# An attention backward kernel: transposing e by one DMA per unit instead of one per two units, with the plain loads and stores on another queue

## Chip, cores and metric

The kernel runs on one core of one Trainium2 chip. The metric is the time of an execution on the device in microseconds (us). One run of the kernel before took 3037.18 us and is left out of every ratio. A ratio is the mean time of one kernel's fast runs over that of the other's of the same rounds on the same chip, so it is not quite the ratio of the medians that are quoted beside it. Each profile is of one of four runs.

## The reference, cut to what matters

The program computes the forward pass and all gradients of two attention blocks over 2048 tokens. The change touches the second one, softmax attention with 16 heads of 28 and one shared key and value head:

```python
def _B_ref(x, wq, wk, wv, wo):
    q = (x @ wq).reshape(B, S, H, Dh).transpose(0, 2, 1, 3)   # 16 query heads
    k, v = x @ wk, x @ wv                                      # one key, one value head
    p = softmax(einsum("bhqd,bkd->bhqk", q, k) * Dh ** -0.5)
    o = einsum("bhqk,bkd->bhqd", p, v)
    return o.transpose(0, 2, 1, 3).reshape(B, S, H * Dh) @ wo
_out, _vjp = jax.vjp(_f, ...)                                  # returned with _vjp(grad_out)
```

The gradient of v needs the exponentials e with queries on the partitions, while the scores are made with keys on the partitions. So all of e, 128 MB of bf16, passes through a transposing DMA.

## The kernel before

A loop of 64 blocks of 8 units does the attention forward and backward together, with the backward part 16 units behind. In a unit ScalarE makes two exponentials (128x512 each, together one half of a tile `eT`) and one PSUM copy, VectorE and GpSimd one product each, TensorE the matmuls. After every second unit SyncE transposes the whole tile, 512 KB, by one DMA. Cuts are marked.

```python
pe_ = tile_pool(name="ceT", bufs=10)      # e, one tile per two units
pn_ = tile_pool(name="ceN", bufs=11)      # e transposed
...
oTs = pm_.tile([P, 256], F32, name="oTs", bufs=1)
nc.gpsimd.memset(oTs[:], 0.0)             # ahead of the loop
...
for u in range(NU + 28):                  # NU = 512
    if u in (2, 4, 6, 8) or u % 64 in (40, 42, 44, 46) and u < 448:
        nc.sync.dma_start(qX[qc][...], qn_d[...])             # 256 KB, four per 64 units
    ...
    if hasS:
        nc.scalar.activation(out=et[:, u % 2, 1, :], in_=sp[1][:, :], func=ACT.Exp, scale=scale)
        if u % 2 == 1:
            en = pn_.tile([P, 16, P], BF16, name="eN")
            nc.sync.dma_start_transpose(en[:, :, :], et[:, :, :, :].rearrange("p a b c -> p (a b c)"))
            eN[u // 2] = en
    if u % 2:
        ...                               # dk matmuls
    else:
        o_dq((u - 2, u - 1), (u - 20, u - 19))
        for n in {2: (0,), 4: (1, 2), 6: (3,)}.get(u % 8, ()):
            if 0 <= (b := u // 8 - 2) < NB:
                dv_mm(b, n // 2, n % 2)   # reads the four eN tiles of block b
    if 512 <= u < 530 and u % 2 == 0:
        post_load((u - 512) // 2)         # on_d, grad_out, B_x for the tail: all SyncE
```

Of the kernel before, what the change touches and what calls it, by code (L numbers as in the profile page):

```python
# [15 lines left out]
DH = 28  # L16
# [8 lines left out]
def kernel(  # L25
# [54 lines left out]
    def mm(out_ap, lhsT, rhs, start=True, stop=True):  # L80
        nc.tensor.matmul(out_ap, lhsT=lhsT, rhs=rhs, start=start, stop=stop, tile_position=(0, 0))  # L81
# [525 lines left out]
    with ExitStack() as cs_:  # L607
# [52 lines left out]
        identF = pp_.tile([P, P], F32, name="identF", bufs=1)  # L660
        make_identity(nc, identF[:])
        oTs = pm_.tile([P, 256], F32, name="oTs", bufs=1)
        nc.gpsimd.memset(oTs[:], 0.0)
        wo = pp_.tile([P, 4, D], BF16, name="wo", bufs=1)
        oTq = {}

# [17 lines left out]
        def out_store(i, c0, c1, ps):  # L684
            if c0 == 0:
                ots[i] = pp_.tile([P, D], BF16, name="ot", bufs=1) if i % 2 else flat(R3)[:, 5120:5120 + D]
            nc.vector.tensor_copy(out=ots[i][:, c0:c1], in_=ps[:, 0:c1 - c0])
            if c1 == D:
                nc.sync.dma_start(out0[i * P:(i + 1) * P, D:2 * D], ots[i])

        def by_tokens(t):
            return t.rearrange("p (t d) -> p t d", d=512)
# [38 lines left out]
        def gwo(n0, n1):  # L731
            for n in range(n0, n1):
                st, g_ = (n // 2, n % 2) if n < 32 else (n % 16, n // 16)
                if st == 0:
                    post[g_] = SB[g_ % 2]
                al = post[g_]
                mm(al[:, 0:D], post["on"][st][:, g_ * P:(g_ + 1) * P], post["gb"][st][:, 0:D], start=(st == 0),
                   stop=(st == NS - 1))
                if st == NS - 1:
                    sb = pd_.tile([P, 2, 512], BF16, name="dsT")[:, 0, 0:D]  # L740
                    nc.scalar.activation(out=sb, in_=al[:, 0:D], func=ACT.Copy)
                    for j in range(4):
                        h = 4 * g_ + j
                        nc.sync.dma_start(out_8[h * DH:(h + 1) * DH, :], sb[32 * j + 1:32 * j + 1 + DH, :])

        GW = [0, 0, 0, 2, 5, 8, 11, 14, 18, 22, 26, 29, 32, 36, 40, 44, 48, 52, 56, 60, 64, 64]
        onps, tps2 = {}, {}

        def due(u, lag):
            b, r = divmod(u - lag, 8)  # L750
            return b if r == 0 and 0 <= b < NB else None
# [9 lines left out]
        def o_norm(b):  # L761
            onp = onps.pop(b)
            qc, pair, g, hp = blk(b)
            if pair == 0:
                onat[qc] = pm_.tile([P, 2, 512], BF16, name="onat")
            ont = onat[qc]
            cs0 = slice(pair * 64, pair * 64 + 64)
            r_ = pw_.tile([P, 2, 2, 1], F32, name="rl")
            os_ = oTs[:, 0:P].rearrange("p (q h c) -> p q h c", q=2, h=2)
            nc.vector.tensor_copy(out=os_, in_=onp[:, :, :, :])  # L770
            nc.vector.reciprocal(out=r_[:], in_=os_[:, :, :, 0:1])
            rl[b] = r_
            onv = ont[:, :, cs0].rearrange("p q (h c) -> p q h c", c=32)
            dnv = do_nat[:, 2 * qc:2 * qc + 2, cs0].rearrange("p q (h c) -> p q h c", c=32)
            nc.gpsimd.tensor_tensor(out=onv, in0=os_, in1=r_[:].to_broadcast([P, 2, 2, 32]),
                                    op=ALU.mult)
            dn = pw_.tile([P, 2, 2, 32], BF16, name="don", bufs=3)
            don[b] = dn
            nc.gpsimd.tensor_tensor(out=dn[:], in0=dnv, in1=r_[:].to_broadcast([P, 2, 2, 32]), op=ALU.mult)
            if pair == 7:  # L780
                nc.sync.dma_start(on_d[qc * 256:(qc + 1) * 256, :].rearrange("(q p) c -> p q c", p=P),
                                  ont[:, :, :])

        def do_o(b):
            qc, pair, g, hp = blk(b)
# [81 lines left out]
        with tc.manual_schedule():  # L867
            tc.keep_in_program_order(nc.scalar.activation(out=ex[:], in_=ex[:], func=ACT.Exp))
            for u in range(NU + 28):
                w = u - 16  # L870
                hasS = u < NU
                hasD = 0 <= w < NU
                if u in (2, 4, 6, 8) or u % 64 in (40, 42, 44, 46) and u < 448:
                    qc, a = ((u - 24) // 64 + 1, (u % 64 - 40) // 2) if u > 20 else (0, (u - 2) // 2)
                    if a == 0:
                        qX[qc] = pq_.tile([P, 4, 2, 512], BF16, name="qX")
                    nc.sync.dma_start(qX[qc][32 * a:32 * a + 32, :, :, :].rearrange("j b s c -> j b (s c)"),
                                      qn_d[qc * 256:(qc + 1) * 256, :].rearrange("(b j s) c -> j b (s c)", b=4, s=2))
                if u == 32:
                    nc.sync.dma_start(wo, wo_d[:, 0:D].rearrange("(g p) c -> p g c", p=P))  # L880
                sp = [SB[(2 * u + h) % 3] for h in range(2)] if hasS else None
                dp = DB if hasD else None
                spare = SB[(2 * u + 2) % 3] if hasS else SB[2]
# [17 lines left out]
                if hasD:  # L901
                    dst = pd_.tile([P, 2, 512], BF16, name="dsT")
                    dsT[w] = dst
                    ew = eT[w // 2]
                    nc.vector.tensor_tensor(out=dst[:, 0, :], in0=dp[0][:, :], in1=ew[:, w % 2, 0, :], op=ALU.mult)  # L905
                    cp = pc_.tile([P, 512], BF16, name="cp")
                    nc.scalar.activation(out=cp[:, :], in_=dp[1][:, :], func=ACT.Copy)  # L907
                    nc.gpsimd.tensor_tensor(out=dst[:, 1, :], in0=cp[:, :], in1=ew[:, w % 2, 1, :], op=ALU.mult)  # L908
                if (b := due(u, 12)) is not None:
                    row_D(b)  # L910
                if (b := due(u, 9)) is not None:
# [17 lines left out]
                    do_copy(*dpj, dps_)  # L929
                if hasS:  # L930
                    nc.scalar.activation(out=et[:, u % 2, 1, :], in_=sp[1][:, :], func=ACT.Exp, scale=scale)  # L931
                    if u % 2 == 1:
                        en = pn_.tile([P, 16, P], BF16, name="eN")
                        nc.sync.dma_start_transpose(en[:, :, :], et[:, :, :, :].rearrange("p a b c -> p (a b c)"))
                        eN[u // 2] = en

                if u % 2:
                    b, i = divmod(u - 27, 8)
# [33 lines left out]
        def gen(i, dt=F32):  # L972
            gens[i % 2] += 1
            t = [SB, DB][i % 2][gens[i % 2] % (3 - i % 2)]
            return t.bitcast(dt) if dt != F32 else t
# [3 lines left out]

        for c in range(4):  # L980
            nc.vector.tensor_copy(out=dkvT[32:64, c * 512:(c + 1) * 512], in_=dv_acc[32 * c:32 * c + 32, :])
            nc.scalar.activation(out=dkvT[0:32, :].rearrange("p (t a i) -> p t a i", a=4, i=32)[:, :, c, :],
                                 in_=dk_acc[32 * c:32 * c + 32, :].rearrange("p (t i) -> p t i", i=32), func=ACT.Copy,
                                 scale=scale)
        def dwq(c):
            r = DC_ROWS[c]
            al = gen(0)
# [2 lines left out]
            sb = sbuf()[:, 0:D].rearrange("p (h e) -> p h e", e=DH)  # L990
            nc.vector.tensor_copy(out=sb[0:r], in_=al[0:r, :].rearrange("p (h c) -> p h c", c=32)[:, :, 1:1 + DH])
            nc.sync.dma_start(out_5[c * P:c * P + r, :].rearrange("r (h e) -> r h e", e=DH), sb[0:r])
        dwq(0)
        for q4 in range(4):
            ps = gen(1, BF16)[:, 0:512].rearrange("p (s k) -> p s k", k=P)
            for s in range(4):
                st = 4 * q4 + s
                nc.tensor.transpose(ps[:, s, :], dkvT[:, st * P:(st + 1) * P], identB[:, :], tile_position=(0, 0))
            nc.vector.tensor_copy(out=dkvn[:, 4 * q4:4 * q4 + 4, :], in_=ps[:, :, 0:64])
        for c in range(4):  # L1000
            r = DC_ROWS[c]
            ps = gen(0)
            for st in range(NS):
                mm(ps[:, 0:64], xb[st][:, c * P:(c + 1) * P], dkvn[:, st, :], start=(st == 0), stop=(st == NS - 1))
            sk = sbuf()[:, 0:2 * DH].rearrange("p (w e) -> p w e", e=DH)
            nc.scalar.activation(out=sk[0:r], in_=ps[0:r, 0:64].rearrange("p (w c) -> p w c", c=32)[:, :, 1:1 + DH],
                                 func=ACT.Copy)
            nc.sync.dma_start(out_6[c * P:c * P + r, :], sk[0:r, 0, :])
            nc.gpsimd.dma_start(out_7[c * P:c * P + r, :], sk[0:r, 1, :])
        for c in range(1, 4):  # L1010
            dwq(c)
        for st in range(NS):
            ps = gen(st)
            for g in range(4):
                mm(ps[:, 0:D], qT_B[g][:, st * P:(st + 1) * P], wqT[:, g, :], start=(g == 0), stop=False)
            mm(ps[:, 0:D], dkvT[:, st * P:(st + 1) * P], wkvT, start=False, stop=True)
            ot = sbuf()[:, 0:D]
            if st % 2:
                nc.vector.tensor_copy(out=ot, in_=ps[:, 0:D])
            else:  # L1020
                nc.scalar.activation(out=ot, in_=ps[:, 0:D], func=ACT.Copy)
            [nc.scalar, nc.sync][st % 2].dma_start(out4[st * P:(st + 1) * P, :], ot)
        psc.close()


# [28 lines left out]
```

## Time and profile before

| | before |
|---|---|
| median of the fast runs | 1124.36 us (1120.13 to 1124.66) |
| span of the profiled run | 1120.9 us |
| until the exponentials of unit 0 are done | 230.3 us |
| from there to those of unit 24 | 38.2 us |
| units 24 to 504 | 753.3 us, 1.569 a unit |
| units 504 to 511 | 10.5 us |
| from there to the end | 88.6 us |

The last five rows are the end times of the second exponential of those units in the trace; they add up to the span. How busy the engines are, what they wait for and where the queue stands is read in the prediction. One line more is the view of one source line, the transposes of e in the kernel before: how many there were, and the minimum, median and maximum time in ns that SyncE's queue (SPq) spent on one.

```profile
L934 SPq DMA_TRANSPOSE eN<-eT x256: 1316/2944/4579, 235.9 to 1038.7; - x128
```

The minimum, 1.32 us, is what a 512 KB transpose costs its issuer when there is room behind it; the median, 2.94, includes the wait for that room.

### The profile page before, as it was taken

What the parts mean: (1) busy time and instruction counts of PE and PEld (TensorE: products, weight loads), DVE (VectorE), ACT (ScalarE), POOL (GpSimd) and SP (SyncE); (2) the same over time, 40 slices, a digit from 0 to 9 for tenths busy, and PEclk for the clock granted to TensorE, in tenths of its full rate; (3) what the DMA queues carried; (4) which work ended last, traced back from release to release, by engine and by line L of the source; (5) the groups of instructions that cost most, each with busy time, mean ns of one, the idle gap of its engine ahead of it and who ended that gap; (6) DMA issues with size and microseconds to landing.
All of it is one profiled execution on the core that took longest, in us unless ns stands there. A gap on an engine that the chain in (4) does not pass through costs nothing.

```text
span 1120.9 us, 42460 instructions
## 1 busy us (share of the span) xinstructions
PE 1054.3 (94%) x17285; PEld 503.6 (45%) x17285; DVE 891.9 (80%) x1770; ACT 878.3 (78%) x1746; POOL 729.8 (65%) x922
## 2 busy tenths in 40 slices
PE   9999999989989999999999899899989999999888
PEld 5545555444434444444444344344434444444344
DVE  7886400428989999999999899899989999999622
ACT  6443122569989999999999899899989999999311
POOL 6001252317878888888888788788878888888500
PEclk9999999989989999999999999999989999999899
DMA  9769899199999999999999999999999999999952
GB/s 267 143 123 183 172 185 214 38 205 189 196 183 192 182 200 184 170 190 196 192 176 197 185 186 179 195 181 183 180 201 192 191 189 194 184 188 180 265 121 78
DMA packets 680725, 203.16 MB, mean 181 GB/s; under 512 B 649713, under 2 KB 675057, under 8 KB 680529
## 3 DMA queue, kind: packets, MB, share of 16 engines
q1 hardware_dynamic: 672656, 190.21, 102.2%
q0 software_dynamic: 2912, 6.28, 1.8%
q10 hardware_dynamic: 4960, 3.96, 1.3%
q8 instruction: 135, 2.21, 0.8%
q14 instruction: 62, 0.50, 0.1%
HBM read 22.83 MB, written 15.03 MB: 34 GB/s over the span
## 4 chain that ended last, share of the span: by engine, by line
PE 66%; DVE 12%; ACT 10%; DMA 7%; issue 2%; SPq 1%; DVEq 0%; ACTq 0%; POOL 0%; POOLq 0%
PE dk_acc L627 18%; PE agen L81 12%; PE sps L627 12%; ACT eT L931 7%; PE oq L627 6%; DMA eN<-eT 5%; PE dps L627 5%; PE aacc L81 4%; DVE dsT L905 4%; PE dv_acc L627 4%; DVE dsx L963 3%; PE sps L81 3%; PE sps L804 1%; DVE R L915 1%; ACT cp L907 1%
## 5 line engine op out<-in xcount | busy, mean ns | idle before, releaser
L908 POOL TENSOR_TENSOR dsT<-cp,eT 128x512 bf16<-128x512 bf16 x512 | 589.8, 1157 | 148.3 <-ACT cp L907 134.7
L905 DVE TENSOR_TENSOR dsT<-dps,eT 128x512 bf16<-128x512 f32 x512 | 341.4, 667 | 39.2 <-PE dps L627 33.7
L627 PEld LDWEIGHTS <-R 32*128 32x128 bf16 (+1 forms) x8704 | 227.7, 94 | 292.7 <-issue 258.8
L963 DVE STREAM_TRANSPOSE dsx<-dsT 128x512 f32<-128x512 f32 x512 | 356.0, 696 | 2.0
L900 ACT ACTIVATE eT<-sps 128x512 bf16<-128x512 f32 x512 | 312.0, 609 | 42.3 <-PE dps L627 23.0
L907 ACT ACTIVATE cp<-dps 128x512 bf16<-128x512 f32 x512 | 312.7, 611 | 17.9 <-PE dps L627 16.9
L931 ACT ACTIVATE eT<-sps 128x512 bf16<-128x512 f32 x512 | 318.8, 623 | 0.0
L627 PE MATMUL dk_acc<-dsx,qX 32*32 32x512 bf16 x4096 | 271.1, 379 | 0.0
L627 PE MATMUL dps<-doT,R 32*128 32x256 bf16 x2048 | 249.5, 271 | 6.2 <-ACT cp L907 1.8
L627 PE MATMUL sps<-R,R 32*128 32x256 bf16 (+1 forms) x2240 | 227.9, 276 | 8.8 <-DVE R L862 1.9
L627 PE MATMUL oq<-eT,R 128*32 128x256 bf16 x2048 | 158.5, 276 | 0.0
L627 PE MATMUL oq<-dsT,R 128*32 128x256 bf16 x2048 | 157.6, 275 | 0.1
L627 PEld LDWEIGHTS <-qX 32*32 32x32 bf16 x4096 | 80.1, 89 | 117.1 <-issue 57.5
L627 PE MATMUL dv_acc<-eN,don 128*32 128x512 bf16 x1024 | 103.4, 385 | 12.8 <-DMA eN<-eT 12.8
L397 POOL MEMSET ga<- 64x448 bf16 x2 | 0.9, 471 | 94.8 <-PE agen L359 81.5
L547 DVE TENSOR_TENSOR osb<-R 32x512 bf16<-32x512 bf16 x4 | 1.7, 413 | 62.1 <-ACT R L544 62.1
L81 PEld LDWEIGHTS <-R 128*128 128x128 bf16 (+1 forms) x361 | 29.7, 99 | 28.2 <-issue 5.3
L627 PE MATMUL sps<-identF,oTs 128*32 128x64 f32 x1024 | 27.8, 226 | 10.7 <-DVE oTs L912 3.4
L627 PEld LDWEIGHTS <-don 128*32 128x32 bf16 x1024 | 34.6, 98 | 0.6
L627 PEld LDWEIGHTS sps<-identF,oTs 128*32 128x32 f32 x1024 | 17.4, 110 | 28.5 <-ACT eT L931 24.7
L81 PE MATMUL agen<-R,R 128*128 128x448 bf16 x128 | 28.6, 352 | 0.8 <-ACT R L220 0.6
L915 DVE TENSOR_SCALAR R<-oq 64x256 bf16<-64x256 f32 x64 | 27.3, 426 | 2.6 <-PE oq L627 0.7
(218 smaller groups left out, 988.8 us busy)
## 6 DMA issues: line engine op xcount, KB each, us to landing
qX<-qn_d SPq DMA_DIRECT2D x32, 256.0 KB
eN<-eT SPq DMA_TRANSPOSE x256
out_dram<-osb ACTq DMA_DIRECT2D x22, 112.0 KB
qn_d<-gaT SPq DMA_DIRECT2D x2, 1024.0 KB
on_d<-onat SPq DMA_DIRECT2D x8, 256.0 KB
xa<-in_A_x_dram SPq DMA_DIRECT2D x8, 224.0 KB
ga<-in_grad_out_dram SPq DMA_DIRECT2D x4, 448.0 KB
xa<-in_grad_out_dram POOLq DMA_DIRECT2D x4, 448.0 KB, 6.1
```

Source lines behind the costliest of these rows:

```text
L81: nc.tensor.matmul(out_ap, lhsT=lhsT, rhs=rhs, start=start, stop=stop, tile_position=(0, 0))
L397: nc.gpsimd.memset(t[64:128, 3, :], 0.0)
L547: nc.vector.tensor_tensor(out=sq[0:32, :], in0=kT[0:32, qc * 512:(qc + 1) * 512], in1=kT[0:32, qc * 512:(qc + 1) * 512], op=ALU.mult)
L627: nc.tensor.matmul(out, lhsT=lhsT, rhs=rhs, start=start, stop=stop, tile_position=pos, skip_group_check=True)
L804: nc.tensor.transpose(tp2[q:q + 32, qb * P:(qb + 1) * P], don[b][:, qb, h, :], identB[:, :], tile_position=(0, q))
L900: nc.scalar.activation(out=et[:, u % 2, 0, :], in_=sp[0][:, :], func=ACT.Exp, scale=scale)
L905: nc.vector.tensor_tensor(out=dst[:, 0, :], in0=dp[0][:, :], in1=ew[:, w % 2, 0, :], op=ALU.mult)
L907: nc.scalar.activation(out=cp[:, :], in_=dp[1][:, :], func=ACT.Copy)
L908: nc.gpsimd.tensor_tensor(out=dst[:, 1, :], in0=cp[:, :], in1=ew[:, w % 2, 1, :], op=ALU.mult)
L915: nc.vector.tensor_scalar(out=qT_B[g][64 * hp:64 * hp + 64, qc * 256:(qc + 1) * 256], in0=oq[64:128, 0:256], scalar1=scale, scalar2=None, ...
L931: nc.scalar.activation(out=et[:, u % 2, 1, :], in_=sp[1][:, :], func=ACT.Exp, scale=scale)
L963: nc.vector.transpose(out=dsx[b][:, tp, :, :, :].rearrange("p h t c -> p (h t c)").bitcast(F32), in_=dsT[y][:, :, :].rearrange("p h c -> p ...
```

## The change

Its intent: start each transpose as soon as its unit is ready, keep SyncE's queue free of everything else, and shorten the tail. Core of the diff, cut:

```diff
-        nc.gpsimd.memset(oTs[:], 0.0)
...
-                if u in (2, 4, 6, 8) or u % 64 in (40, 42, 44, 46) and u < 448:
-                    ...
-                    nc.sync.dma_start(qX[qc][...], qn_d[...])
...
+                if u in (2, 4, 6, 8) or u % 64 in (30, 38, 46, 54) and u < 448:
+                    ...
+                    nc.gpsimd.dma_start(qX[qc][...], qn_d[...])
+                if u == 4:
+                    nc.vector.memset(oTs[64:128, :], 0.0)
...
-                    if u % 2 == 1:
-                        en = pn_.tile([P, 16, P], BF16, name="eN")
-                        nc.sync.dma_start_transpose(en[:, :, :], et[:, :, :, :].rearrange("p a b c -> p (a b c)"))
-                        eN[u // 2] = en
+                    if u % 2 == 0:
+                        eN[u // 2] = pn_.tile([P, 16, P], BF16, name="eN")
+                    nc.sync.dma_start_transpose(eN[u // 2][:, 8 * (u % 2):8 * (u % 2) + 8, :],
+                                                et[:, u % 2, :, :].rearrange("p b c -> p (b c)"))
```

The stores of on_d, out_0 and out_8 and the load of wo go to GpSimd's queue as well. In the tail, six of the dx tiles come before the gradients of wk, wv and wq, the scaling of dk is shared between ScalarE and VectorE, and the dwo matmuls take slightly later slots. Below, S is the split, G the loads and stores on GpSimd, M the moved memset, T the tail.

More of the change, by code (lines that the diff above doesn't have):

```diff
@@ L688, in out_store @@
             if c1 == D:
-                nc.sync.dma_start(out0[i * P:(i + 1) * P, D:2 * D], ots[i])
+                nc.gpsimd.dma_start(out0[i * P:(i + 1) * P, D:2 * D], ots[i])
         def by_tokens(t):
@@ L743, in gwo @@
                         h = 4 * g_ + j
-                        nc.sync.dma_start(out_8[h * DH:(h + 1) * DH, :], sb[32 * j + 1:32 * j + 1 + DH, :])
-        GW = [0, 0, 0, 2, 5, 8, 11, 14, 18, 22, 26, 29, 32, 36, 40, 44, 48, 52, 56, 60, 64, 64]
+                        nc.gpsimd.dma_start(out_8[h * DH:(h + 1) * DH, :], sb[32 * j + 1:32 * j + 1 + DH, :])
+        GW = [0, 0, 0, 0, 4, 8, 12, 16, 19, 22, 26, 29, 32, 36, 40, 44, 48, 52, 56, 60, 64, 64]
         onps, tps2 = {}, {}
@@ L779, in o_norm @@
             nc.gpsimd.tensor_tensor(out=dn[:], in0=dnv, in1=r_[:].to_broadcast([P, 2, 2, 32]), op=ALU.mult)
-            if pair == 7:
-                nc.sync.dma_start(on_d[qc * 256:(qc + 1) * 256, :].rearrange("(q p) c -> p q c", p=P),
-                                  ont[:, :, :])
         def do_o(b):
@@ L872 @@
                 hasD = 0 <= w < NU
-                if u in (2, 4, 6, 8) or u % 64 in (40, 42, 44, 46) and u < 448:
-                    qc, a = ((u - 24) // 64 + 1, (u % 64 - 40) // 2) if u > 20 else (0, (u - 2) // 2)
-                    if a == 0:
-                        qX[qc] = pq_.tile([P, 4, 2, 512], BF16, name="qX")
-                    nc.sync.dma_start(qX[qc][32 * a:32 * a + 32, :, :, :].rearrange("j b s c -> j b (s c)"),
-                                      qn_d[qc * 256:(qc + 1) * 256, :].rearrange("(b j s) c -> j b (s c)", b=4, s=2))
-                if u == 32:
-                    nc.sync.dma_start(wo, wo_d[:, 0:D].rearrange("(g p) c -> p g c", p=P))
                 sp = [SB[(2 * u + h) % 3] for h in range(2)] if hasS else None
@@ L908 @@
                     nc.gpsimd.tensor_tensor(out=dst[:, 1, :], in0=cp[:, :], in1=ew[:, w % 2, 1, :], op=ALU.mult)
+                if u in (2, 4, 6, 8) or u % 64 in (30, 38, 46, 54) and u < 448:
+                    qc, a = (u // 64 + 1, (u % 64 - 30) // 8) if u > 20 else (0, (u - 2) // 2)
+                    if a == 0:
+                        qX[qc] = pq_.tile([P, 4, 2, 512], BF16, name="qX")
+                    nc.gpsimd.dma_start(qX[qc][32 * a:32 * a + 32, :, :, :].rearrange("j b s c -> j b (s c)"),
+                                        qn_d[qc * 256:(qc + 1) * 256, :].rearrange("(b j s) c -> j b (s c)", b=4, s=2))
+                if u == 12:
+                    nc.gpsimd.dma_start(wo, wo_d[:, 0:D].rearrange("(g p) c -> p g c", p=P))
+                if u == 4:
+                    nc.vector.memset(oTs[64:128, :], 0.0)
+                if (b := due(u, 14)) is not None and b % 8 == 7 and b < NB - 1:
+                    nc.gpsimd.dma_start(on_d[b // 8 * 256:(b // 8 + 1) * 256, :].rearrange("(q p) c -> p q c", p=P),
+                                        onat[b // 8][:, :, :])
                 if (b := due(u, 12)) is not None:
@@ L981 @@
             nc.vector.tensor_copy(out=dkvT[32:64, c * 512:(c + 1) * 512], in_=dv_acc[32 * c:32 * c + 32, :])
-            nc.scalar.activation(out=dkvT[0:32, :].rearrange("p (t a i) -> p t a i", a=4, i=32)[:, :, c, :],
-                                 in_=dk_acc[32 * c:32 * c + 32, :].rearrange("p (t i) -> p t i", i=32), func=ACT.Copy,
-                                 scale=scale)
+        for c in range(4):
+            t = dkvT[0:32, :].rearrange("p (t a i) -> p t a i", a=4, i=32)[:, :, c, :]
+            src = dk_acc[32 * c:32 * c + 32, :].rearrange("p (t i) -> p t i", i=32)
+            if c % 2:
+                nc.vector.tensor_scalar(out=t, in0=src, scalar1=scale, scalar2=None, op0=ALU.mult)
+            else:
+                nc.scalar.activation(out=t, in_=src, func=ACT.Copy, scale=scale)
         def dwq(c):
@@ L992, in dwq, with dkv_T @@
             nc.sync.dma_start(out_5[c * P:c * P + r, :].rearrange("r (h e) -> r h e", e=DH), sb[0:r])
-        dwq(0)
-        for q4 in range(4):
+        def dkv_T(q4):
             ps = gen(1, BF16)[:, 0:512].rearrange("p (s k) -> p s k", k=P)
@@ L999, with dx @@
             nc.vector.tensor_copy(out=dkvn[:, 4 * q4:4 * q4 + 4, :], in_=ps[:, :, 0:64])
+        def dx(st):
+            ps = gen(st)
+            for g in range(4):
+                mm(ps[:, 0:D], qT_B[g][:, st * P:(st + 1) * P], wqT[:, g, :], start=(g == 0), stop=False)
+            mm(ps[:, 0:D], dkvT[:, st * P:(st + 1) * P], wkvT, start=False, stop=True)
+            ot = sbuf()[:, 0:D]
+            if st % 2:
+                nc.vector.tensor_copy(out=ot, in_=ps[:, 0:D])
+            else:
+                nc.scalar.activation(out=ot, in_=ps[:, 0:D], func=ACT.Copy)
+            [nc.scalar, nc.sync][st % 2].dma_start(out4[st * P:(st + 1) * P, :], ot)
+        for st in range(6):
+            dx(st)
+            if 0 < st < 5:
+                dkv_T(st - 1)
         for c in range(4):
@@ L1009 @@
             nc.gpsimd.dma_start(out_7[c * P:c * P + r, :], sk[0:r, 1, :])
-        for c in range(1, 4):
+        for c in range(4):
             dwq(c)
-        for st in range(NS):
-            ps = gen(st)
-            for g in range(4):
-                mm(ps[:, 0:D], qT_B[g][:, st * P:(st + 1) * P], wqT[:, g, :], start=(g == 0), stop=False)
-            mm(ps[:, 0:D], dkvT[:, st * P:(st + 1) * P], wkvT, start=False, stop=True)
-            ot = sbuf()[:, 0:D]
-            if st % 2:
-                nc.vector.tensor_copy(out=ot, in_=ps[:, 0:D])
-            else:
-                nc.scalar.activation(out=ot, in_=ps[:, 0:D], func=ACT.Copy)
-            [nc.scalar, nc.sync][st % 2].dma_start(out4[st * P:(st + 1) * P, :], ot)
+        for st in range(6, NS):
+            dx(st)
         psc.close()
```

## The prediction

> **What bounds the kernel now.** I read the page, then the waits, the windows of busy time, and the timeline at the loop's start, inside it and at the end. The loop (64 blocks of 8 units, from about 229 to 1040 us) is close to a tie. In its best stretch ScalarE is 98.9% busy, in others 93 to 94%:
>
> ```profile
> 400.00:500.00 100.00, 95.83 (x1996) 45.97 (x1992) 96.91 (x189) 98.29 (x197) 85.15 (x101) 1.00 1.19 184
> 700.00:800.00 100.00, 92.84 (x1829) 42.19 (x1828) 91.97 (x176) 93.46 (x188) 81.38 (x94) 0.98 1.15 183
> 800.00:900.00 100.00, 93.91 (x1860) 43.07 (x1864) 92.22 (x177) 94.25 (x189) 81.84 (x96) 0.97 1.18 193
> 900.00:1000.00 100.00, 96.12 (x1956) 44.83 (x1955) 96.91 (x187) 98.92 (x199) 85.43 (x98) 1.00 1.20 190
> ```
>
> Columns: stretch, length, busy time of PE, weight loads, DVE, ACT, POOL, then granted clock and DMA. At three ACT instructions a unit, 199 is 66.3 units in 100 us, 1.51 us each; 188 is 1.60. What takes the rest is in the waits:
>
> ```profile
> ACT eT L900 <- PE dps L627: 22.4, 26, 3.3
> PE dv_acc L627 <- DMA eN<-eT: 12.8, 10, 2.5
> ```
>
> TensorE waits ten times, 12.8 us, for the transposed e; ScalarE then loses 22.4 us behind it. The difference is the clock. After the longest wait the granted clock was 0.50 for about 6 us, and the sixteen dk matmuls took 1.89 instead of 1.05 us:
>
> ```profile
> 827.76 0.59 PE L627 MATMUL dv_acc<-eN,don 128*32 128x512 bf16 x1 [2.53 <-DMA eN<-eT]
> 828.82 1.89 PE L627 MATMUL dk_acc<-dsx,qX 32*32 32x512 bf16 x16
> 836.66 1.05 PE L627 MATMUL dk_acc<-dsx,qX 32*32 32x512 bf16 x16
> ```
>
> Mean clocks of 0.97, 0.98 and 0.97 in three windows of 100 us (300 to 400 is the third) mean about 16 us at half speed, 8 us of work. So 12.8 + 8 = 21 us, which agrees with ScalarE's 22.4. The e transposes are late because SyncE's queue is never empty:
>
> ```profile
> 1027.99 13.10 SPq L934 DMA_TRANSPOSE eN<-eT  x5
> 1031.64 0.60 ACT L931 ACTIVATE eT<-sps 128x512 bf16<-128x512 f32 x1
> ...
> 606.65 3.10 SPq L934 DMA_TRANSPOSE eN<-eT  x1
> 609.80 0.58 SPq L877 DMA_DIRECT2D qX<-qn_d  x1
> 610.49 2.81 SPq L934 DMA_TRANSPOSE eN<-eT  x1
> ```
>
> The last e is written at 1032.2, its transpose leaves SyncE at 1041.1: 8.8 us of backlog even at the end. Near 606 each qX load adds 0.7 us to a pair of units. Every 64 units (on_d stores at 749.5, 849.5, 949.6) take 100 us, the queue's own pace: 1.56 us a unit.
>
> **What the Trainium skill says.** "DMA: Bandwidth & Descriptors", section "Issuing engines are not separate DMA queues": DMAs of all issuers run on the same 16 engines, and a second issuer saves only sequencer time. The trace agrees that data is the larger part: a 512 KB transpose left SyncE in 1.3 us when the queue had room, but a full queue takes four in 9.69 us, 2.42 us each, and 2.6 to 3.0 in the loop. The same page, "Latency and other measured facts", gives 261 GB/s for a DMA transpose; 512 KB in 2.42 us is 217 here, so the measurement is used. "TensorE: Matmul & The Clock Gate", Part 1, says an idle window of about 3.4 us halves the clock and sustained work restores it; the halved clock above agrees, though here a wait of 2.53 us was enough. These pages make me expect that moving qX does not remove its bytes, but that an absent wait is worth nearly twice its length.
>
> **The change, part by part.**
>
> Two transposes for one. The bytes are the same, the instructions double to 512. The issue floor hardly depends on size, as four 256 KB transposes before the loop show (1.40 us each with gaps), against 1.33 for 512 KB:
>
> ```profile
> 219.38 5.59 SPq L580 DMA_TRANSPOSE gaT<-R  x4
> 1073.22 9.69 SPq L955 DMA_TRANSPOSE dsx<-R  x4
> ```
>
> SyncE thus needs 1.40 us a unit at least. Data needs half of 2.85 us (the middle of 2.6 to 3.0), 1.43, plus what shares the engines: in 64 units four qX loads of about 0.8 us, three stores of about 0.5, one 256 KB transpose of 1.4, together 6.1 us or 0.10 a unit. That is 1.53 against 1.51 to 1.53 that the compute engines need. It is a tie again, but two things tip it. In the present queue each load stands between transposes, here also for its 0.1 us gaps and latency. And the start empties the queue: now four qX loads sit between the first transposes and the first wait for qn_d's store until 244.5, so the loop begins with about 14 us of backlog. Then transposes go on behind the store while the engines stall, and I expect a backlog near 3 us. dv needs eN 11 units (about 16.5 us) after the last e of its block, so some 13 us of slack remain; over 500 units that tolerates 1.55 us a unit without a wait. I count 80% of the 21 us: minus 17.
>
> Loads and stores on GpSimd. About 44 issues of 0.55 to 0.78 us, as GpSimd's plain DMAs cost before the loop, make some 30 us. GpSimd was idle for 148 us in front of its L908, and qX is spread to one load a block. Zero on the path.
>
> The oTs memset. Now GpSimd waits for the qn_d store and everything stops at unit 10:
>
> ```profile
> 239.22 0.46 SPq L581 DMA_DIRECT2D qn_d<-gaT  x1
> 244.57 0.31 POOL L663 MEMSET oTs<- 128x256 f32 x1 [15.82 <-DMA qn_d<-gaT]
> 244.91 0.42 DVE L912 COPY oTs<-oq 64x256 f32<-64x256 f32 x1 [4.22 <-POOL oTs L663]
> ```
>
> The changed program's order has the memset on VectorE at unit 4, waiting for that same store. The PSUM copies behind it are then late, and TensorE stops at unit 6, whose projection needs the bank that the copy of unit 4 frees. The store is not earlier. Four units are lost; two such units took 2.36 us, so plus 4.7 us.
>
> The end of the loop. TensorE waits 3.96 us for the on_d load behind the backlog, and runs at a clock of 0.51 for the next 6.4 us, 3.2 us of work:
>
> ```profile
> 1045.00:1049.60 4.60, 0.65 (x12) 0.10 (x5) 1.03 (x2) 0.77 (x2) 1.57 (x2) 0.94 1.31 206
> 1049.60:1056.00 6.40, 6.40 (x42) 1.72 (x43) 3.01 (x5) 1.50 (x3) 2.11 (x2) 0.51 1.05 295
> ```
>
> With a shorter backlog, and the first of these matmuls one unit later, the wait goes: minus 7.2 us.
>
> The tail. Eight stores of 24.5 KB stood before the four dq transposes (3.7 us), and TensorE waited 0.9 us for the scaled dk and 2.2 us for the transposes. Six dx tiles of 0.95 us each, which need neither, now come first, dk's scaling is shared with VectorE, and the stores are on GpSimd: minus 3.0 us. The dx work itself is only moved.
>
> Sum: -17 + 4.7 - 7.2 - 3.0 = -22.5 us on 1124.66, which is 1102; with all of the 21 us it is 1098. I put 1101.
>
> **The rivals.** (a) The transposes become issue-bound. A floor of 1.40 us with nothing left to hide a DMA stall: in the four 256 KB ones the queue's pace was up to 1.50 us (6.02 us for the second four, partly waiting). For it: the page's DMA row shows nine tenths throughout. At 1.60 us a unit the backlog reaches 13 us after some 170 units (0.075 a unit), and the other 340 pay 0.075 each, 25 us: the old loss comes back, and the time is about 1124 + 4 + 4.7 - 7 - 3 = 1123. Against it: half-size transposes leave in 1.25 us, and the loop's own data rate, not its issue, is what filled the queue. (b) GpSimd becomes a bound. Its work per block is 8 x 1.157 + 1.45 = 10.7 us, plus 0.7 for a DMA, 11.4 of 12.2. It is against this rival that the slack stays positive, but don (L796) is already waited for 24 times; a load that delays it could cost TensorE 0.5 us in 28 blocks, 14 us: 1115. (c) All waits go, and with them all the half-speed work: 1098, or 1094 if the start is not worse.
>
> **Range and chances.** The loop's 21 us decides. Two chances in three that most of it goes (1094 to 1104), one in four that half stays (1104 to 1114), the rest that rival (a) or (b) takes it (1114 to 1125). The end and tail, 10 us, are nearly sure, the start's 4.7 us quite likely. The limit for "faster" is 1102.2, in the middle of the likeliest case: 0.55 faster, 0.41 the same, 0.04 slower. Range 1090 to 1118.
>
> **What would show each step.** Right: the wait of dv_acc for eN vanishes or falls under 3 us; the clock stays 1.00 from 260 us to the end; the last transpose leaves SyncE under 5 us after the last exp; 64 units take 97 to 98 us; ScalarE's idle time behind dps falls by 20 us; VectorE sits 5 to 7 us before the new memset; no wait for on_d at 1045 and none for the dq transposes. Wrong: SyncE's transposes take 1.5 us or more each with a backlog that grows through the loop and waits that gather in its second half (rival a); new waits on GpSimd's don or dsT (rival b); or a start that does not lose four units, because the copies are not blocked by the memset.

## The result, and the profile after

| | before | after |
|---|---|---|
| median of the fast runs | 1124.36 us | 1167.04 us (1164.36 to 1169.98) |
| ratio | | 1.0392, 95% interval [1.0346, 1.0439] |
| span of the profiled run | 1120.9 | 1167.0 |
| until unit 0 | 230.3 | 232.5 |
| to unit 24 | 38.2 | 47.5 |
| units 24 to 504 | 753.3, 1.569 a unit | 790.1, 1.646 a unit |
| units 504 to 511 | 10.5 | 10.5 |
| to the end | 88.6 | 86.4 |

The changed kernel is slower by 3.9%, where 2% faster had been the centre. The differences of the last five rows add up to the 46.1 us between the spans: 36.8 are in the steady loop, 9.3 in its first 24 units, 2.2 before it (where the program is the same, and other runs spread from 227.7 to 232.7), and the tail is 2.2 better.

The windows of busy time after, with the columns that the prediction explains:

```profile
400.00:500.00 100.00, 91.04 (x1864) 43.65 (x1860) 90.99 (x175) 91.78 (x185) 83.37 (x99) 1.00 1.18 172
700.00:800.00 100.00, 92.33 (x1819) 41.95 (x1808) 91.08 (x174) 92.27 (x185) 84.37 (x102) 0.98 1.19 182
800.00:900.00 100.00, 90.56 (x1765) 41.16 (x1763) 88.40 (x169) 89.86 (x181) 81.59 (x95) 0.97 1.18 176
900.00:1000.00 100.00, 91.74 (x1788) 41.47 (x1784) 89.25 (x171) 89.89 (x181) 82.83 (x98) 0.97 1.18 178
```

ScalarE, the engine that was up to 98.9% busy, is now at 90 to 92% in these four windows. What it waits for has not changed in kind, only in size (waits of the whole trace: in total us, times, longest; the first was 23.0 us in 29 waits before):

```profile
ACT eT L888 <- PE dps L627: 59.0, 50, 3.9
PE dv_acc L627 <- DMA eN<-eT: 39.4, 27, 3.1
```

TensorE now waits 27 times for the transposed e instead of ten, and three times as long in all. The whole stretch from 300 to 1000 us, before and then after, in the same columns:

```profile
300.00:1000.00 700.00, 659.94 (x13288) 306.95 (x13280) 658.39 (x1262) 669.32 (x1337) 580.09 (x667) 0.99 1.18 188
```

```profile
300.00:1000.00 700.00, 639.44 (x12641) 294.90 (x12636) 629.85 (x1201) 636.70 (x1272) 579.63 (x681) 0.98 1.18 177
```

The DMA engines move 177 GB/s instead of 188, yet their busy share, the last but one number, stays at 1.18. So that share does not tell a queue that is full of data from one that is not. The view of the transposes' source line tells more:

```profile
L935 SPq DMA_TRANSPOSE eN<-eT x512: 1231/1296/5192, 237.9 to 1092.3; - x171
```

For half the bytes the minimum is 1.23 us, against 1.32 before, and the median is 1.30: most transposes now take just the time of an issue. With the 0.1 us to the next one that is 1.40 us a unit, as the prediction had it, but the queue does not keep this pace. SyncE's timeline in the middle of the loop and at its end, and TensorE's at the end (start, duration, then what; several of a kind are joined into one line):

```profile
558.97 11.57 SPq L935 DMA_TRANSPOSE eN<-eT  x7
570.63 1.29 SPq L924 DMA_TRANSPOSE oTq<-onat  x1
572.02 7.91 SPq L935 DMA_TRANSPOSE eN<-eT  x5
...
1083.98 10.57 SPq L935 DMA_TRANSPOSE eN<-eT  x7
...
1101.25 1.67 PE L81 MATMUL sps<-eT,eN 128*128 128x448 bf16 x4 [4.17 <-DMA eN<-on_d]
```

Seven transposes in 11.57 us are 1.65 each, five in 7.91 are 1.58, the last seven 1.51. The last exponential ends at 1080.6 and the last transpose leaves SyncE at 1094.6, 14 us later; in the kernel before it was 8.8. So the wait for on_d, which stands behind the transposes, stays: 4.17 us, not zero.

The start of the loop, with lines of SyncE, VectorE and TensorE:

```profile
241.84 0.46 SPq L581 DMA_DIRECT2D qn_d<-gaT  x1
...
247.17 0.27 DVE L906 MEMSET oTs<- 64x256 f32 x1 [9.98 <-DMA qn_d<-gaT]
...
247.95 1.04 PE L627 MATMUL dps<-R,R 128*32 128x256 bf16 x16 [8.38 <-DVE R L858]
```

The store that the memset waits for was issued 2.6 us later than before (241.84 against 239.22 in the prediction's lines), and TensorE stops for 8.38 us behind VectorE's 9.98.

### The profile page after: what moved, and what is told of

The parts are those of the page before. It is cut to its first block, busy times and chain, and to the rows that moved or that the text cites. A ratio compares the mean times of both kernels' runs of the same rounds, so it can differ in the third digit from the quotient of the medians.

```text
span 1167.0 us, 43106 instructions
## 1 busy us (share of the span) xinstructions
PE 1070.4 (92%) x17280; PEld 508.7 (44%) x17285; DVE 897.0 (77%) x1773; ACT 877.0 (75%) x1744; POOL 770.6 (66%) x993
## 3 DMA queue, kind: packets, MB, share of 16 engines
q8 instruction: 135, 2.21, 0.8%
## 4 chain that ended last, share of the span: by engine, by line
PE 64%; DMA 17%; ACT 8%; DVE 6%; issue 2%; POOL 1%; SPq 0%; DVEq 0%; ACTq 0%; POOLq 0%
PE dk_acc L627 17%; DMA eN<-eT 15%; PE agen L81 12%; PE sps L627 10%; ACT eT L932 6%; PE oq L627 6%; PE dps L627 5%; PE dv_acc L627 4%; PE aacc L81 4%; PE sps L81 3%; DVE dsT L893 2%; DVE dsx L964 2%; PE sps L800 1%; ACT cp L895 1%; PE dps L81 1%
## 5 line engine op out<-in xcount | busy, mean ns | idle before, releaser
L627 PE MATMUL dk_acc<-dsx,qX 32*32 32x512 bf16 x4096 | 274.7, 384 | 0.0
L627 PE MATMUL dps<-doT,R 32*128 32x256 bf16 x2048 | 252.6, 274 | 5.3 <-ACT cp L895 2.0
L627 PE MATMUL dv_acc<-eN,don 128*32 128x512 bf16 x1024 | 112.2, 385 | 39.7 <-DMA eN<-eT 39.4
L627 PEld LDWEIGHTS <-don 128*32 128x32 bf16 x1024 | 37.6, 98 | 47.6 <-DMA eN<-eT 46.9
L901 POOL DMA_DIRECT2D qX<-qn_d x32 | 18.6, 581 | 17.0 <-DMA qn_d<-gaT 17.0
L774 POOL TENSOR_TENSOR onat<-oTs,rl 128x128 bf16<-128x128 f32 x64 | 25.7, 401 | 5.9 <-DVE rl L770 5.9
```

The lines of the kernel that those rows point to most:

```text
L627: nc.tensor.matmul(out, lhsT=lhsT, rhs=rhs, start=start, stop=stop, tile_position=pos, skip_group_check=True)
L774: nc.gpsimd.tensor_tensor(out=onv, in0=os_, in1=r_[:].to_broadcast([P, 2, 2, 32]), op=ALU.mult)
L901: nc.gpsimd.dma_start(qX[qc][32 * a:32 * a + 32, :, :, :].rearrange("j b s c -> j b (s c)"), qn_d[qc * 256:(qc + 1) * 256, :].rearrange("( ...
```

## The experiments

The main theory after the comparison: the split (S) makes the transposes bound by their issue, and a pause in the transfers can no longer be made up. The rivals: G disturbs the transposes, or M's loss at the start is what costs.

### The split alone

```diff
-  (one transpose per two units)
+  (one transpose per unit, as in the change; all else as before)
```

> The kernel before with one part of the change alone: one 256 KB transpose of e per unit. Loads, stores, the oTs memset and the tail stay. Theory A (the split makes the transposes issue-bound: 1.28 us in the issue plus 0.1, and a stall of the transfers can no longer be made up): 1.62 to 1.70 us a unit, some 25 waits of dv_acc for eN of 30 us or more, 1150 to 1175 us. Theory B (the loads and stores on GpSimd's queue disturb the transposes) and theory C (the loss at the loop's start, from the moved memset): nothing of either is in here, so 1115 to 1130 us.

Measured: 1173.13 us median, ratio 1.046 [1.0432, 1.0488]; 40.1 us for the first 24 units, 1.656 a unit after them. Its waits and its transposes:

```profile
PE dv_acc L627 <- DMA eN<-eT: 41.5, 25, 3.7
...
L934 SPq DMA_TRANSPOSE eN<-eT x512: 1231/1291/2669, 235.2 to 1086.4; - x171
```

The split alone has all of the loss, and more. GpSimd's queue and the memset are not needed for it.

### The changed kernel with the split undone

```diff
-                    nc.sync.dma_start_transpose(eN[u // 2][:, 8 * (u % 2):8 * (u % 2) + 8, :], ...)
+                    if u % 2 == 1:
+                        nc.sync.dma_start_transpose(en[:, :, :], ...)       # 512 KB
```

> The changed kernel with the split undone: one 512 KB transpose per two units, everything else as changed. Theory A: the time falls under that of before, 1105 to 1120 us (the loads have left the queue, the tail gains some 3 us, the start still costs 5 to 10), with a backlog of SyncE that is under 5 us in the loop. Theory B: 1145 us or more, since the loads are still on GpSimd. Theory C: the start costs 9 us, and the rest of the loss stays small: 1130 to 1140.

Measured: 1115.78 us, ratio 0.9956 [0.9909, 1.0002]; first 24 units 43.3 us, 1.549 a unit. The waits, and the window from 300 to 1000 us:

```profile
PE dv_acc L627 <- DMA eN<-eT: 7.8, 10, 1.2
...
300.00:1000.00 700.00, 664.65 (x13474) 310.58 (x13472) 667.69 (x1280) 678.94 (x1356) 615.09 (x726) 1.00 1.20 189
```

The time is within what theory A said. The backlog is not: over the last seven eighths of the loop nine in ten transposes leave SyncE 9.3 to 14.0 us behind the exponential they read last, not under 5 (8.8 to 15.7 before, 11.0 to 16.5 in the changed kernel). Nor is SyncE ever idle from 300 to 1000 us, in this run or in any other: from the end of one issue to the start of the next it is never more than 0.5 us. So the queue of 512 KB transposes has no time to spare either; its pace is only close to that of the engines.

### The loads and stores on GpSimd alone

```diff
-                    nc.sync.dma_start(qX[qc][...], qn_d[...])          # at u % 64 in (40, 42, 44, 46)
+                    nc.gpsimd.dma_start(qX[qc][...], qn_d[...])        # at u % 64 in (30, 38, 46, 54)
   (wo, on_d, out_0, out_8 too, as in the change; the rest as before)
```

> The kernel before with the plain loads and stores of the loop on GpSimd's queue at the changed kernel's places, the memset, the two-unit transposes and the tail as before. Theory A: 1108 to 1122 us, fewer waits of dv_acc for eN than the ten of before. Theory B: over 1140 us, with transposes that take longer wherever a qX load runs.

Measured: 1112.17 us, ratio 0.9924 [0.9868, 0.998]; 1.547 us a unit, and six waits of dv_acc for eN, 6.0 us. This part of the change helps by itself, so theory B falls.

### The changed kernel with the loads and stores back on SyncE

```diff
-                    nc.gpsimd.dma_start(...)
+                    nc.sync.dma_start(...)            # at the places of before; S, M, T as changed
```

> The changed kernel with the plain loads and stores back on SyncE's queue at the places of before; split, memset and tail as changed. Theory A: as slow as the changed kernel or slower, 1160 to 1180 us, because the loads now take issue time in a queue that is bound by issue. Theory B: 1120 to 1135 us.

Measured: 1165.53 us, ratio 1.04 [1.0366, 1.0434]; 1.652 a unit. As theory A said: with the split in, it hardly matters where the loads are.

### The same bytes, cut unevenly: 480 KB and 32 KB

Is it the number of transposes that counts, or that their data come in smaller pieces?

```diff
-                        nc.sync.dma_start_transpose(en[:, :, :], flat_e)
+                        nc.sync.dma_start_transpose(en[:, 0:15, :], flat_e[:, 0:1920])
+                        nc.sync.dma_start_transpose(en[:, 15:16, :], flat_e[:, 1920:2048])
```

> The kernel before, each 512 KB transpose of e cut unevenly into 480 KB and 32 KB, both issued one after the other when the pair of units is ready; the same bytes and the same 512 instructions as the even split, in another place. Theory A1 (a transpose holds SyncE's queue for some 1.25 us plus 0.1 whatever its size): as slow as the even split, 1.63 to 1.67 us a unit in the loop and 1155 to 1175 us, and the 32 KB transposes show 1.1 us or more each. Theory A2 (what costs is the transfer of many small pieces, or that each unit's data now move at another moment): a 32 KB transpose then costs some 0.2 to 0.4 us, and the time is 1122 to 1135 us.

Measured: 1345.11 us, ratio 1.1979 [1.1953, 1.2005]; 2.002 us a unit. A2 falls, since the small transposes show over 1.2 us each. But A1 falls short too: it gave at most 1175. The timeline of SyncE, where L935 is the 480 KB piece and L936 the 32 KB piece, and the window from 300 to 1000 us:

```profile
600.37 1.62 SPq L935 DMA_TRANSPOSE eN<-eT  x1
602.03 1.81 SPq L936 DMA_TRANSPOSE eN<-eT  x1
603.94 1.59 SPq L935 DMA_TRANSPOSE eN<-eT  x1
605.59 1.84 SPq L936 DMA_TRANSPOSE eN<-eT  x1
607.53 2.14 SPq L935 DMA_TRANSPOSE eN<-eT  x1
...
300.00:1000.00 700.00, 569.97 (x10460) 244.42 (x10456) 526.72 (x993) 527.67 (x1049) 458.49 (x525) 0.90 0.87 148
```

The small piece occupies SyncE longer than the large one, and a pair takes 3.57 us from 600.37 to 603.94. In this run the DMA share falls to 0.87: the engines have nothing to move for a part of each pair. In the trace no packet of a transpose starts from 604.19 to 605.13, although the issue of the next 480 KB began at 603.94: the first comes 1.2 us after that start. From 300 to 1000 us such gaps of over 0.3 us add up to 200 us, against 82 in the kernel before (and only 49 in the changed kernel, where two even halves leave few gaps).

This suggests two stages. SyncE prepares a transpose for about 1.23 us, whichever of these sizes it has; then its data move, 2.4 to 2.5 us per 512 KB, and only the preparation of the next one runs beside them. A 32 KB piece can't leave SyncE before the 480 KB ahead of it have moved: 1.23 + 15/16 x 2.42 = 3.5 us from the first start, as the timeline shows (1.62 + 0.04 + 1.81 = 3.47). After it, the preparation of the next large piece has only 32 KB to hide it.

### 384 KB and 128 KB

The two-stage theory was put to a cut of another ratio, against the count theory:

```diff
-                        nc.sync.dma_start_transpose(en[:, :, :], flat_e)
+                        nc.sync.dma_start_transpose(en[:, 0:12, :], flat_e[:, 0:1536])
+                        nc.sync.dma_start_transpose(en[:, 12:16, :], flat_e[:, 1536:2048])
```

> The kernel before, each 512 KB transpose of e cut into 384 KB and 128 KB, issued one after the other. It tells apart two forms of the issue theory, after the cut into 480 and 32 KB took 1345 us where 1155 to 1175 had been expected. Two-stage theory (SyncE needs 1.23 us to prepare a transpose, whatever its size; its data, 2.5 us per 512 KB, move after that, and only beside the preparation of the next one; so a pair of pieces takes the larger of 1.23 and the other piece's data, twice, plus 0.2): floor 1.23 + 1.88 + 0.2 = 3.3 us a pair of units; with the 10% that the uneven cut had above its floor (4.0 against 1.23 + 2.35 + 0.1) 3.6, so 1.80 us a unit and 1225 to 1250 us. Count theory (each transpose costs 1.25 plus 0.1, and only their number matters): 1.65 us a unit, 1160 to 1180 us, and then the uneven cut was slow for another reason, such as a 32 KB transpose that uses few engines.

Measured: 1252.2 us (1243.94 to 1256.58), ratio 1.1153 [1.1097, 1.1209]; 1.824 us a unit. The median is 2 us above the range of the two-stage theory, and 72 above that of the count theory. The two source lines, 384 KB first:

```profile
L935 SPq DMA_TRANSPOSE eN<-eT x256: 1278/1462/2967, 235.8 to 1169.8; - x128
L936 SPq DMA_TRANSPOSE eN<-eT x256: 1202/1554/2640, 238.5 to 1171.4; - x128
```

The minima, 1.20 us for 128 KB and 1.28 for 384, fit a preparation that hardly depends on size. The medians add up to 3.02, and 1.23 + 3/4 x 2.42 is 3.05. The four cuts side by side, per pair of units; the floor is what preparation and data give without any pause, with the 0.1 to 0.2 us between instructions, and the measured column is twice the loop's time a unit:

| pieces, KB | floor, us | measured, us | run |
|---|---|---|---|
| 512 | 2.42 + 0.1 = 2.5 | 3.09 | loads on GpSimd alone |
| 256 + 256 | 2 x 1.30 + 0.2 = 2.8 | 3.29 | the changed kernel |
| 384 + 128 | 1.23 + 1.82 + 0.2 = 3.25 | 3.65 | this one |
| 480 + 32 | 1.23 + 2.27 + 0.14 = 3.64 | 4.00 | the uneven cut |

All four run 0.36 to 0.6 us above their floors (in the last two, loads on SyncE are in it). The packets in the traces tell where most of this excess lies. The table below takes the pairs of units from 300 to 1000 us that have no other SyncE transfer between them, each timed from its first issue to that of the next pair. It parts them by whether a fetch of instructions (a 16 KB packet of DMA queue q8, which the page calls "instruction"; 1.02 to 1.11 us on the mean) begins within the pair or up to 1.3 us before it:

| pieces, KB | run | without a fetch: mean us (pairs) | with a fetch |
|---|---|---|---|
| 512 | loads on GpSimd alone | 2.41 (98) | 3.52 (122) |
| 256 + 256 | the split alone | 2.78 (71) | 3.38 (91) |
| 256 + 256 | the changed kernel | 2.93 (89) | 3.54 (113) |
| 384 + 128 | this one | 3.22 (72) | 3.65 (79) |
| 480 + 32 | the uneven cut | 3.60 (69) | 3.87 (66) |

Without a fetch the pairs take their floors to within 0.15 us, and a pause comes on top in every cut. That a fetch causes it is not shown: this is a coincidence in time. A 512 KB transpose does not hide the pause either, since pairs with a fetch take about 3.5 us in the first and the third row. What the split adds lies in the other pairs, 2.8 to 2.9 us instead of 2.4. With 512 KB the measured 3.09 is close to the 3.02 to 3.06 that the prediction took the engines to need for a pair. With two even halves, 3.29 is well over it.

### Three more microseconds of slack

If single pauses beyond the slack cost the time, more slack would help.

```diff
-                    for n in {2: (0,), 4: (1, 2), 6: (3,)}.get(u % 8, ()):
-                        if 0 <= (b := u // 8 - 2) < NB:
+                    for n in {4: (0,), 6: (1, 2), 0: (3,)}.get(u % 8, ()):
+                        if 0 <= (b := (u - 2) // 8 - 2) < NB:
```

> The changed kernel with the four dv matmul groups of a block two units (3 us) later, so that TensorE asks for the transposed e 13 units after the block's last e instead of 11. Rate theory (the split queue needs more time a unit than the engines): 3 us of slack are used up once, after some 30 units, and the loop keeps 1.63 to 1.66 us a unit: 1158 to 1167 us. Rival (the queue's mean rate would do, and single stalls longer than the slack cost the time): most of the 27 waits, 3.1 us at most and 1.5 on the mean, go: 1125 to 1145 us.

Measured: 1167.3 us, ratio 1.0418 [1.036, 1.0476]; 1.646 a unit, exactly that of the changed kernel. The rate theory had 1158 to 1167, the rival at most 1145.

```profile
PE dv_acc L627 <- DMA eN<-eT: 41.6, 38, 2.6
```

The waits become more and shorter; their sum stays. In its new place dv also meets VectorE (27 waits of TensorE for dsT, 8.9 us), but the waits for eN alone speak for the rate theory: the queue is bound by its rate.

### The memset put back

```diff
+        nc.gpsimd.memset(oTs[:], 0.0)                        # ahead of the loop
-                if u == 4:
-                    nc.vector.memset(oTs[64:128, :], 0.0)    # S, G, T as changed
```

> The changed kernel with the oTs memset put back on GpSimd ahead of the loop. If the moved memset is what lengthens the first 24 units (38.2 us before, 47.5 in the profile of the changed kernel), they take 38 to 41 us here and the time is 5 to 8 us under the changed kernel, 1158 to 1163 us. If the loss at the start is only borrowed from the loop, which is bound by the transposes anyway, the time stays at 1165 to 1170.

Measured: 1171.25 us (1162.37 to 1172.48), ratio 1.0407 [1.0366, 1.0448]. In the profile the first 24 units take 39.2 us instead of 47.5, and the loop 1.655 a unit instead of 1.646. The start is mended, and the time is not better; it lies above both expected ranges. A loop bound by its queue takes the gain back, or the spread of the runs hides it: the profiled run is the fastest of the four, by 9 us. Over all profiles, the four kernels with the moved memset need 42.8 to 47.5 us for the first 24 units (mean 45.2), the nine with the old memset and the old oTs tile 38.2 to 42.5 (mean 39.8).

### The tail alone

```diff
   (dx tiles first, dk's scaling shared, later dwo slots, as in the change; all else as before)
```

> The kernel before with the changed tail alone (dx tiles first, dk's scaling shared with VectorE, the other slots of the dwo matmuls). The prediction's step: 3 us less than before, 1117 to 1120 us, as the waits for the dq transposes and for the scaled dk go. Rival: what is left of the tail is bound by something that both orders share (the last stores, the on_d wait), and the time is that of before within 1 us.

Measured: 1116.67 us, ratio 0.9938 [0.9923, 0.9953]: 7 us, twice what was expected. The stretch after the last exponential falls from 88.6 to 82.8 us. In the kernel before TensorE's waits after 1030 us include the two below. In this run neither is listed in the tail, and the wait for on_d is 1.7 us instead of 4.0:

```profile
PE sps L81 <- DMA dsx<-R: 2.2, 1, 2.2
...
PE dps L998 <- ACT qX L982: 0.9, 1, 0.9
```

### Three tries at a faster version

First, before plus G, with oTs in a pool whose memory no late store reads, later first qX loads, and on_d loaded by GpSimd:

```diff
-        oTs = pm_.tile([P, 256], F32, name="oTs", bufs=1)
+        oTs = pp_.tile([P, 256], F32, name="oTs", bufs=1)
-                if u in (2, 4, 6, 8) or ...                       # qX
+                if u in (11, 12, 13, 14) or ...
-                nc.sync.dma_start(t[:, 0:n, :], on_d[...])
+                nc.gpsimd.dma_start(t[:, 0:n, :], on_d[...])
```

> A version meant to beat both: before, with the plain loads and stores on GpSimd (as in the run that had them alone, 1112 us), oTs in a pool whose memory no late store reads, so that its memset waits for nothing, qX loads of the first block after unit 10, and the on_d loads of the end on GpSimd too, so that they don't stand behind the transposes. Expected: the first 24 units in 35 to 37 us, no wait for on_d at the end (3 to 4 us, and the half clock behind it), 1100 to 1106 us. Rival: the start only hands its gain to the queue, which then holds the loop up: 1108 to 1112 us.

Measured: 1122.86 us, ratio 0.9979 [0.9931, 1.0026], above both expected ranges. Both gains were lost at the next wait, one at each end of the loop:

```profile
263.05 0.58 PE L627 MATMUL dv_acc<-eN,don 128*32 128x512 bf16 x1 [3.20 <-DMA eN<-eT]
...
PE sps L81 <- DMA eT<-in_grad_out_dram: 6.2, 1, 6.2
```

It seems that the stall at the start had let the queue catch up; without it dv_acc waits for eN, and the first 24 units take 41.6 us. At the end, on_d comes in time, but the load of grad_out beside it still stands behind the transposes.

Second, G and T together:

```diff
   (the changed kernel with 512 KB transposes and with the old memset)
```

> The changed kernel without its two costly parts: one transpose per two units, the oTs memset on GpSimd ahead of the loop; loads and stores on GpSimd and the new tail stay. Single parts gave 9 us (loads) and 7 us (tail) against before. If they add: 1105 to 1108 us. If both gained by the same thing at the loop's end (the tail alone took 82.8 us after the last exp, the loads alone 84.3, before 88.6): 1109 to 1113.

Measured: 1116.89 us, ratio 0.9963 [0.9923, 1.0004], above both expected ranges. The gains of G (0.76%) and T (0.62%) do not add; the stretch after the last exponential is 81.6 us, which T alone and G alone (84.3) nearly had.

Third, the same with dv two units later and the first loads of the loop's end on GpSimd:

```diff
   (as the run above, with the dv slots of the slack experiment)
-                nc.sync.dma_start(...)                        # grad_out and on_d, first two of each
+                nc.gpsimd.dma_start(...)
```

> A version meant to beat both: the run above (one transpose per two units, memset as before, loads on GpSimd, new tail) with the dv groups two units later and the first four loads of the loop's end (grad_out and on_d) on GpSimd, so that they don't stand behind the transposes. Where the queue's mean rate is enough, 3 us more slack takes away nearly all waits of dv_acc for eN (ten, 1.3 us each, in before) and the half clock behind them: 1.53 us a unit, 1094 to 1102 us. If the queue is bound by its rate here too, the waits come back later: 1104 to 1110.

Measured: 1121.41 us, ratio 0.9996 [0.9958, 1.0034], above both expected ranges. The waits for eN fall to five, 5.7 us, as expected; but in dv's new place TensorE meets VectorE instead:

```profile
PE dps L627 <- DVE dsT L894: 18.7, 53, 0.6
PE dv_acc L627 <- DMA eN<-eT: 5.7, 5, 2.2
```

The fastest are thus G alone and T alone, each some 0.7% under before, which is within 2%.

## Why the prediction was wrong

**The bound.** That ScalarE loses its time behind TensorE, and TensorE behind the transposed e, held in every run but the last: there TensorE waited more for VectorE (18.7 us) than for e (5.7).

**Two transposes for one: the step that failed.** The prediction put SyncE's need at 1.40 us a unit and the data's at 1.43 plus 0.10, "a tie again" at 1.53. The 1.40 was right: the median issue was 1.30 plus 0.1. What failed is treating issue and data as two limits of which the larger counts. The 1.43 already held the pauses of the transfers, the 1.40 held none. The measured need was 1.646: a 256 KB transpose has 1.2 us of data against 1.30 + 0.1 of issue, so the issue is the floor, and the pauses come on top of it. They come on top with 512 KB as well; what the split cost is the higher floor, 2.78 to 2.93 us a pair instead of 2.41 where no fetch interferes. The split alone (1.656 a unit) and the split undone (1.549) show that the split is what costs, the two uneven cuts that its issue does. The 13 us of slack did not help: "tolerates 1.55" may have been right, but the queue needed 1.65, and 3 us more gained nothing. Instead of minus 17 us, the steady loop cost plus 37 in the profile.

**Rival (a)** named this mechanism, "a floor of 1.40 us with nothing left to hide a DMA stall" (though 512 KB did not hide one either). Its pace of 1.60 was mis-sized, 1.646 in the profile, and so was its result: it took the queue to lose about what the loop had lost before. The argument against it, that half-size transposes leave in 1.25 us, was none: 1.25 is the issue itself. The chance of 0.04 for slower was the cost of that. Its signs came in part: the transposes took 1.54 us each on the mean from 300 to 1000 us, but the backlog stayed near 14 us after the first eighth of the loop, and 10 of the 27 waits fell in its first half.

**Loads on GpSimd, and rival (b).** No cost on the path: right. Alone they brought 0.76%. GpSimd never became the bound; it is busy 83% of 300 to 1000 us in the changed kernel.

**The memset.** Plus 4.7 us; 9.3 in the profile of the changed kernel, 5.4 as the mean over the kernels with and without it. The mechanism, TensorE stopped behind VectorE's wait for the qn_d store, is in the trace. In the total it did not show.

**The end of the loop.** Minus 7.2 us; nothing came in the changed kernel. It rested on a short backlog, which was 14 us. Even with the split undone, TensorE still waited 3.3 us for on_d.

**The tail.** Minus 3.0 us; alone 7 by the ratio, 5.8 in the profile. The two waits that it named, 3.1 us, went. Some 2.3 us more came from the wait for on_d, which the later dwo slots shorten in that profile and which the prediction had booked under the end of the loop.

**What stays open.** Why the transposes pause was not settled. The pauses coincide with the instruction fetches of q8, about 0.47 for every pair of units in every run; in the kernel before these are 135 packets and 2.21 MB in all, 64 bytes for each of TensorE's 34,570 instructions, so they are probably TensorE's. No experiment took them away: this was seen and not shown. Issuing the two halves from two queues, which might hide one preparation behind the other, was not tried: the Trainium skill, "DMA: Bandwidth & Descriptors", section "Silent corruption: two transposing streams in flight at once", says that transposes of two streams in flight together can silently corrupt both outputs. No run here shows that. Nor is the two-stage form shown beyond these four cuts of one tile.

## What to carry to other kernels

Before a transfer is split, write down its preparation and its data separately, both without pauses, take the larger, and add the pauses to that. Here the data of 256 KB, 1.2 us, no longer outlasted the preparation of the next, 1.3, and the issue became the bound. If a transfer must be split, equal pieces were the least bad of the three cuts tried, and 480 + 32 KB the worst. A busy DMA row does not tell the two states apart; the minimum and median time of the issuing instruction, and the bytes per second, do.

## What the Trainium skill lacked or had wrong

- "DMA: Bandwidth & Descriptors", "Issuing engines are not separate DMA queues", calls the sequencer's time to initiate a DMA usually small beside the DMA itself. For a DMA transpose it is not: the shortest seen were 1.22 us for 32 KB, 1.20 for 128, 1.23 for 256 and 1.32 for 512, where 256 KB of data take 1.2 us. The page's only figures for it, in the section "Why a DMA increments its semaphore by 16 and not by 1", are in sequencer cycles for "previous generations", none of them for 32 to 512 KB from SBUF to SBUF.
- No page says how the preparation of one transpose and the data of the one before overlap. The runs show 1345 us for pieces of 480 + 32 KB, 1252 for 384 + 128, 1166 to 1173 for 256 + 256, and 1112 to 1124 for one of 512.
- "DMA: Bandwidth & Descriptors", "Latency and other measured facts", gives 261 GB/s for a DMA transpose with a non-contiguous middle dimension and 350 to 400 for the contiguous case; a full queue of 512 KB transposes held 217 here (2.42 us each).
- "TensorE: Matmul & The Clock Gate", Part 1, gives an idle window of about 3.4 us for the clock's halving; here the clock fell to 0.50 some 2.0 us into an idle time of TensorE of 2.53 us (at 827.2 us in the kernel before).
